# Attention beside an MLP on one core: where the transposed scores stand behind a value product

## The chip, the core and the metric

The kernel runs on one core of a Trainium2 chip. The metric is the device time of one execution in microseconds (us). Differences under about 0.2% (1.6 us) cannot be told from no change.

## What is computed

Inputs are float32: a sequence `x` of 2048 rows by 512 columns, attention weights for 32 heads of 16, and an MLP with 1792 hidden columns. The two branches are mixed by a gate computed for each row:

```
qkv = x @ wqkv                         # 32 heads, Dh = 16
scores = q k^T * Dh**-0.5              # row i sees columns i-255 .. i
a = (softmax(scores) @ v) @ wo
b = (silu(x @ w_gate) * (x @ w_up)) @ w_down
out = g * a + (1 - g) * b              # g = sigmoid(sum(x * gate_w)) per row
```

## The kernel before

Every float32 factor of the projections is split into a high and a low half, and three products of the halves are summed. The program has three stages: projections of q, k, v and a part of the MLP (0 to about 168 us); the attention stage, in which the rest of the MLP's gate and up products fill TensorE between the attention's own (about 168 to 633 us); and the output stage. The change lies in the second.

The 32 heads make 8 groups of four (`G`), the sequence 16 blocks of 128 rows (`NB`). The main loop runs over 128 slots `t`, one for each head group and key block, and each slot has four **places** `hd`. What stands in a place is written out by hand, and every engine executes its queue in that order:

- one **score** (`run(scores, 1)`, function `stage1`, L603): a matmul with 63 rows of weights into a PSUM bank of `pc` (three banks in turn, `pb1` among them), read by VectorE, which takes the row maximum for the next head group (L605).
- one **transposed score** (function `stage2`, L642) into a bank of `pd` (two banks in turn), read by ScalarE, which exponentiates it into `pt` (L644). GpSimd then masks pairs of them (L646, L649).
- some **steps** of the MLP products (`run(steps, n)`, function `lanes`, L564). A step is two matmuls with 64 rows of weights each, one on the upper and one on the lower half of TensorE's rows. Twelve steps complete a sum; ScalarE then copies it to `ev` (L511, function `copy_out`), in its own queue behind what the same place issued before.

A score and a transposed score use one half of the rows each: `r = slice(64 * j, ...)`, with `j` alternating from one to the next. `stage2` takes its heads in the order 1, 0, 3, 2 and the scores run one ahead, so that in a place of the kernel before both stand on the same half.

Every fourth slot has, after the steps of its second place, a **value product** (`av`, L664): 32 or 48 calls that multiply the exponentials of the last four to six key blocks by the values, into one bank of `pc` and one of `pd` (in the last head group two of `pc`). ScalarE copies the `pd` bank out (`ob`, L675) and VectorE the `pc` bank (`oe`, L681); after that the two banks go back into their turns. The table `DEAL` gives the steps of each place in the four slots from one value product's slot to the next.

Below, the 16 places of four slots are numbered 0 to 15, and such four slots are called a round. The value product stands at the end of place 1, and place 2 is the first behind it. T2 is the transposed score that the kernel before issues in place 2, T3 the next, and so on; the names stay with the scores in both kernels.

Of the kernel before, what the change touches and what calls it, by code (L numbers as in the profile page):

```python
# [19 lines left out]
NB = S // P  # L20
CH = 512
NCH = S // CH
G = H // 4
NF = F // P
VW = 4 * (DH + 1) + DH
NSLOT = 4
# [7 lines left out]
def gated_mix(ctx, tc, xT, xn, wqk, wv, wo, wgu, wd, gw, out):  # L34
# [52 lines left out]
    def run(gen, n=None):  # L87

        while n is None or n > 0:
            if next(gen, run) is run:  # L90
                break
            n = n and n - 1
# [19 lines left out]
    def bank(n):  # L112
        names = BANKS[n if isinstance(n, str) else ("pa", "pb", "pc", "pd")[n]]
        names.append(names.pop(0))
        return psum.tile([P, CH], F32, name=names[-1])
# [353 lines left out]
    with ExitStack() as A:  # L469
# [30 lines left out]
        def tick_end():  # L500
            for f in AT.pop(NOW[0], ()):
                f()
# [88 lines left out]
        def stage1(g, qb):  # L591

            hf, b = divmod(qb, NB // 2)
            if b == 0:
                MX[g, hf] = sm.tile([P, 4, NB // 2], F32, name="mx")
            q0, k0 = qb * P, max(0, qb - 2) * P
            n = q0 + P - k0
            for hd in range(4):
                pr, j = divmod(hd, 2)
                r = slice(64 * j, 64 * j + 63)  # L600

                ps = bank("pd") if g == 0 and pr else bank("pc")
                nc.tensor.matmul(ps[:, :n], QT[g % 2][pr][r, q0:q0 + P], KT[g % 2][pr][r, k0:k0 + n],  # L603
                                 start=True, stop=True)
                mx = nc.vector.tensor_tensor_reduce(out=ps[:, :n], in0=ps[:, :n], in1=mask[:, 3 * P - n:],  # L605
                                                    scale=1.0, scalar=NEG, op0=ALU.add, op1=ALU.max,
                                                    accum_out=MX[g, hf][:, hd, b:b + 1])
                if g == 0:
                    BEHIND.append(mx)
                yield  # L610

        def put_max(g, hf):

            mt = sm.tile([P, 32], F32R, name="mt", bufs=1)
            mtt = sm.tile([P, 32], F32, name="mtt", bufs=1)
            nc.vector.tensor_scalar(mt, MX[g, hf].rearrange("p h b -> p (h b)"), -1.0, None, op0=ALU.mult)
            nc.vector.transpose(mtt, mt.bitcast(F32))
            md = dram.tile([4, NB // 2, 4, 32], F32, name=f"md{g}{hf}")
            nc.sync.dma_start(md.rearrange("h b p q -> p (h b) q"), mtt)
            for pr in range(2):  # L620
                nc.sync.dma_start(halves_of(QT[g % 2][pr])[hf][63::64].bitcast(F32),
                                  md[2 * pr:2 * pr + 2].rearrange("h b p q -> h (b p q)"))
# [3 lines left out]
        def load_v(n):  # L626

            VG[n] = sm.tile([P, 4, VW], F32, name="vg", bufs=4)
            nc.sync.dma_start(VG[n], vd[n // 4, :, n % 4 * 4:n % 4 * 4 + 4])

        def stage2(g, kb):


            n = min(3, NB - kb) * P
            k0 = kb * P
            for hd in (1, 0, 3, 2):
                pr, j = divmod(hd, 2)
                r = slice(64 * j, 64 * j + 64)
                if j:
                    pt = PT[g, kb, pr] = ptp.tile([P, 2, 3 * P], F32, name="pt")  # L640
                ps = bank("pd")
                nc.tensor.matmul(ps[:, :n], KT[g % 2][pr][r, k0:k0 + P], QT[g % 2][pr][r, k0:k0 + n],  # L642
                                 start=True, stop=True)
                BEHIND.append(nc.scalar.activation(pt[:, j, :n], ps[:, :n], AF.Exp, scale=SCALE))  # L644
                if not j:
                    nc.gpsimd.affine_select(out=pt[:, :, :P], in_=pt[:, :, :P], pattern=[[0, 2], [1, P]],  # L646
                                            compare_op=ALU.is_ge, fill=0.0, base=0, channel_multiplier=-1)
                    if n == 3 * P:
                        nc.gpsimd.affine_select(out=pt[:, :, 2 * P:], in_=pt[:, :, 2 * P:],  # L649
                                                pattern=[[0, 2], [-1, P]], compare_op=ALU.is_ge, fill=0.0,  # L650
                                                base=-1, channel_multiplier=1)
                yield

        def av(g, c):

            AV[g, c] = bank("pc"), bank("pc" if g == G - 1 or g == G - 2 and c == NCH - 1 else "pd")

            orders = [[4 * c + m for m in ms if 4 * c + m >= 0] for ms in ((0, 1, 2, -1, -2, 3), (0, 1, -1, 2, 3, -2))]
            for n, kbs in enumerate(zip(*orders)):
                for j in range(4):  # L660
                    for h, (o, kb) in enumerate(zip(HALVES, kbs)):
                        k0 = kb * P + 64 * h
                        q0, q1 = max(k0, c * CH), min(k0 + W + 64, c * CH + CH)
                        nc.tensor.matmul(AV[g, c][h][32 * j:32 * j + 32, q0 - c * CH:q1 - c * CH],  # L664
                                         VG[4 * g + kb // 4][o, kb % 4, 17 * j:17 * j + 32],
                                         PT[g, kb, j // 2][o, j % 2, q0 - kb * P:q1 - kb * P],
                                         start=n == 0, stop=n == len(orders[0]) - 1, skip_group_check=True)

        def evacuate(g, c):

            first, second = AV[g, c]
            lo = 0 if c else 64
            e = osb.tile([P, CH], F32, name="oe", bufs=2)
            o = osb.tile([P, CH], F32, name="ob")
            nc.scalar.copy(o[:, lo:], second[:, lo:])  # L675
            if g == G - 1:
                nc.vector.tensor_tensor(out=e[:, lo:], in0=first[:, lo:], in1=o[:, lo:], op=ALU.add)
                if lo:
                    nc.vector.tensor_copy(e[:, :lo], first[:, :lo])
            else:  # L680
                nc.vector.tensor_copy(e, first)  # L681
                nc.gpsimd.tensor_tensor(out=e[:, lo:], in0=e[:, lo:], in1=o[:, lo:], op=ALU.add)  # L682
            later(4 if g == G - 1 else 0, lambda: nc.gpsimd.dma_start(od[g, :, c * CH:(c + 1) * CH], e))
# [73 lines left out]
        def tile_silu(n):  # L757
            (gt, up), sg = GOT[n], kept()
            TILE[n] = halves_of(pieces[TILE_AT[n]])
            nc.scalar.activation(sg, gt, AF.Silu)  # L760
            nc.vector.tensor_tensor(out=sg, in0=up, in1=sg, op=ALU.mult)
            yield
            split(*TILE[n], sg, nc.scalar, nc.vector)
# [38 lines left out]
            spread(4 * (16 * g + 9) + 3, 1, stack(g + 2, 0))  # L802
            spread(4 * (16 * g + 17) + 1, 1, stack(g + 2, 1))

        DEAL = [[[(hd + 1) * n // 4 - hd * n // 4 for hd in range(4)] for n in deal] for deal in ((5, 9, 8, 8), (8, 8, 8, 8))]
        DEAL[0][0] = 1, 2, 2, 0
        scores = chain(*(stage1(*divmod(b, NB)) for b in range(NB, G * NB)))
        run(scores, 1)
        for t in range(G * NB + 1):
            g, i = divmod(t, NB)  # L810
            d, part = divmod(t, NSLOT)
            s2 = stage2(g, i) if t < G * NB else iter(())
            values = part == 0 and t > 0
            if t == g7:
                BANKS["pc"].remove("pb1")
                BANKS["pd"].append("pb1")
            for hd in range(4):
                k = NOW[0] = NSLOT * t + hd
                run(scores, 1)
                if t < g7:  # L820
                    run(s2, 1)
                elif hd % 2 == 0:
                    run(s2, 2)
                if t == G * NB and hd == 0:
                    last_tile = tile_silu(2)
                    run(last_tile, 1)
                if t < G * NB:
                    run(steps, DEAL[t >= g7][part][hd])
                if hd == 1 and values:
                    av(*divmod(d - 1, NCH))  # L830
                    for f in LULL.pop(k, []) + UNDER:
                        f()
                    UNDER.clear()
                    evacuate(*divmod(d - 1, NCH))
                tick_end()
            if i in (7, 15) and g + 1 < G:
                UNDER.append(lambda g=g, i=i: put_max(g + 1, i // 8))
            if t >= 10 and t % 4 == 2 and t + 6 < G * NB:
                load_v((t + 6) // 4)
# [195 lines left out]
```

## Time and profile before

| what | value |
|---|---|
| median of 3 runs | 822.5 us (822.34 to 822.65) |
| the profiled execution's own time | 822.11 us |
| its span, first to last instruction | 820.4 us |
| busy: TensorE matmuls, weight loads | 812.0 us, 681.0 us |
| busy: VectorE, ScalarE, GpSimd | 550.4 us, 470.0 us, 402.1 us |
| granted TensorE clock | 1.00 |
| from the value product at 392.14 us to the next, at 405.09 us | 12.95 us |

PE is TensorE's matmul row and PEld its weight loads, DVE is VectorE, ACT ScalarE, POOL GpSimd. L603 is line 603 of the kernel. A tile's name in the profile is without its number. In a timeline a row gives the start, the duration, the engine, the line, and the tile written and read; in brackets stands how long the engine's queue was empty or held before it and what released it. Matmul durations run from the start to a modelled end and overlap with the next matmul's.

### The profile page before, as it was taken

Reading aid. Unit: us, or ns where it says so; the run is one execution under the profiler, and the core shown is the slowest. Engines: PE = TensorE matmul, PEld = TensorE weight load, DVE = VectorE, ACT = ScalarE, POOL = GpSimd, SP = SyncE. Lnnn points to the kernel's source line nnn. Section 1 sums busy time; section 2 is a strip of 40 time slices with the busy share of each in tenths; the row PEclk is TensorE's granted clock in tenths of the full one; section 3 lists DMA queues with packets and bytes.
Section 4 is the critical chain, followed back from the end, with each engine's and each line's share of the span. In section 5 each row is a group of like instructions: output and inputs, shape, how many; then the busy total and the mean of one; then the engine's idle time right before and its main releaser. Section 6 shows DMA issues by size and latency. Waiting matters only on the chain.

```text
span 820.4 us, 20498 instructions
## 1 busy us (share of the span) xinstructions
PE 812.0 (99%) x7681; PEld 681.0 (83%) x7681; DVE 550.4 (67%) x1425; ACT 470.0 (57%) x956; POOL 402.1 (49%) x715
## 2 busy tenths in 40 slices
PE   9999999999999999999999999999999999999997
PEld 7888888878888888888888888888887888888886
DVE  5675554248877888878888887786576666554652
ACT  7455553312576767767677676776776563435340
POOL 5124442260366666767667576665873205442320
PEclk9999999999999999999999999999999999999999
DMA  8446666385625654566555655352659997878611
GB/s 302 148 156 254 231 231 235 137 268 178 218 85 194 189 179 157 182 213 202 171 167 168 207 188 159 132 170 89 212 191 349 271 287 229 273 226 221 213 52 52
DMA packets 80211, 159.70 MB, mean 195 GB/s; under 512 B 14960, under 2 KB 19440, under 8 KB 80112
## 3 DMA queue, kind: packets, MB, share of 16 engines
q1 hardware_dynamic: 68544, 127.44, 47.5%
q0 software_dynamic: 10992, 29.91, 11.3%
q8 instruction: 60, 0.98, 0.5%
q10 hardware_dynamic: 576, 1.05, 0.4%
q14 instruction: 39, 0.32, 0.1%
HBM read 93.32 MB, written 65.01 MB: 193 GB/s over the span
## 4 chain that ended last, share of the span: by engine, by line
PE 95%; DMA 2%; DVE 1%; ACT 1%; POOL 0%; SPq 0%; issue 0%; DVEq 0%; ACTq 0%
PE pa L564 22%; PE pb L564 10%; PE pd L642 6%; PE pc L664 5%; PE pd L381 4%; PE pb L381 4%; PE pa L381 4%; PE pd L81 3%; PE pc L81 3%; PE pc L83 3%; PE pd L83 3%; PE pc L82 3%; PE pd L82 3%; PE pb L664 2%; PE pc L381 2%; PE pb L83 2%
## 5 line engine op out<-in xcount | busy, mean ns | idle before, releaser
L644 ACT ACTIVATE pt<-pd 128x384 f32<-128x384 f32 (+2 forms) x491 | 223.0, 474 | 43.9 <-PE pd L642 25.6
L605 DVE CUSTOM_DVE_ANT_0 pc<-pc,mask 128x384 f32<-128x384 f32 (+2 forms) x322 | 173.2, 548 | 23.5 <-PE pc L603 9.6
L642 PE MATMUL pd<-q,k 64*128 64x384 f32 (+2 forms) x491 | 167.2, 348 | 1.8 <-ACT pt L644 1.8
L564 PE MATMUL pa<-xhi,wh 64*128 64x512 f32 x492 | 168.5, 395 | 0.0
L564 PE MATMUL pa<-xlo,wh 64*128 64x512 f32 x492 | 167.6, 394 | 0.0
L564 PE MATMUL pa<-xhi,wl 64*128 64x512 f32 x492 | 165.9, 395 | 0.0
L646 POOL TENSOR_SCALAR_AFFINE_SELECT pt<-pt 128x256 f32<-128x256 f32 x256 | 110.9, 434 | 67.9 <-ACT pt L644 62.7
L642 PEld LDWEIGHTS pd<-q,k 64*128 64x128 f32 x491 | 90.8, 185 | 26.1 <-ACT pt L644 9.8
L603 PE MATMUL pc<-k,q 63*128 63x384 f32 (+2 forms) x322 | 106.9, 337 | 0.0
L564 PE MATMUL pb<-xhi,wl 64*128 64x512 f32 x244 | 96.2, 394 | 0.0
L564 PE MATMUL pb<-xhi,wh 64*128 64x512 f32 x244 | 96.2, 394 | 0.0
L564 PE MATMUL pb<-xlo,wh 64*128 64x512 f32 x244 | 96.2, 394 | 0.0
L649 POOL TENSOR_SCALAR_AFFINE_SELECT pt<-pt 128x256 f32<-128x256 f32 x224 | 94.3, 421 | 0.0
L605 DVE CUSTOM_DVE_ANT_0 pb<-pb,mask 128x384 f32<-128x384 f32 (+2 forms) x158 | 86.9, 550 | 6.9 <-PE pb L603 3.0
L564 PEld LDWEIGHTS pa<-xhi,wh 64*128 64x128 f32 x492 | 88.2, 185 | 1.9 <-DVE mx L605 0.5
L564 PEld LDWEIGHTS pa<-xhi,wl 64*128 64x128 f32 x492 | 87.0, 185 | 1.1
L564 PEld LDWEIGHTS pa<-xlo,wh 64*128 64x128 f32 x492 | 86.9, 185 | 0.6
L605 DVE DVE_READ_ACCUMULATOR2_ANT mx<- 128x1 f32 x512 | 72.8, 142 | 0.0
L921 DVE TENSOR_TENSOR sg<-got,sg 128x512 f32<-128x512 f32 x52 | 41.1, 790 | 45.2 <-ACT sg L920 39.4
L664 PE MATMUL pd<-pt,vg 64*32 64x320 f32 (+4 forms) x1184 | 63.1, 346 | 0.0
L603 PEld LDWEIGHTS pc<-k,q 63*128 63x128 f32 x322 | 58.6, 184 | 4.8 <-issue 4.3
L682 POOL TENSOR_TENSOR oe<-oe,ob 128x512 f32<-128x512 f32 (+1 forms) x28 | 35.2, 1256 | 54.5 <-ACT ob L675 51.5
(307 smaller groups left out, 2050.8 us busy)
## 6 DMA issues: line engine op xcount, KB each, us to landing
got<-raws SPq DMA_DIRECT2D x104, 256.0 KB
raws<-ev SPq DMA_DIRECT2D x91, 256.0 KB
q<-xd SPq DMA_DIRECT2D x96, 128.0 KB
k<-xd SPq DMA_DIRECT2D x96, 128.0 KB
xd<-cx SPq DMA_DIRECT2D x16, 512.0 KB
xd<-cy SPq DMA_DIRECT2D x16, 512.0 KB
od<-oe POOLq DMA_DIRECT2D x32, 256.0 KB, 3.4
raw<-wgu SPq DMA_DIRECT2D x25, 256.0 KB
```

The source lines that it names most:

```text
L81: nc.tensor.matmul(ps, lh, rh, start=start and i == 0, stop=False, skip_group_check=skip)
L82: nc.tensor.matmul(ps, lh, rl, start=False, stop=False, skip_group_check=skip)
L83: nc.tensor.matmul(ps, ll, rh, start=False, stop=stop and i == n - 1, skip_group_check=skip)
L381: nc.tensor.matmul(ps, l[:, w], r[:, k], start=n in (1, 2, 5) and k == m == 0, stop=k == 1 and m == 2, skip_group_check=True)
L564: mm = nc.tensor.matmul(ps[o], w[r], x[r], start=first and i == 0, stop=(o is odd or bool(lane)) and i == turn - 1)
L603: nc.tensor.matmul(ps[:, :n], QT[g % 2][pr][r, q0:q0 + P], KT[g % 2][pr][r, k0:k0 + n], start=True, stop=True)
L605: mx = nc.vector.tensor_tensor_reduce(out=ps[:, :n], in0=ps[:, :n], in1=mask[:, 3 * P - n:], scale=1.0, scalar=NEG, op0=ALU.add, op1=ALU.m ...
L642: nc.tensor.matmul(ps[:, :n], KT[g % 2][pr][r, k0:k0 + P], QT[g % 2][pr][r, k0:k0 + n], start=True, stop=True)
L644: BEHIND.append(nc.scalar.activation(pt[:, j, :n], ps[:, :n], AF.Exp, scale=SCALE))
L646: nc.gpsimd.affine_select(out=pt[:, :, :P], in_=pt[:, :, :P], pattern=[[0, 2], [1, P]], compare_op=ALU.is_ge, fill=0.0, base=0, channel_mu ...
L649: nc.gpsimd.affine_select(out=pt[:, :, 2 * P:], in_=pt[:, :, 2 * P:], pattern=[[0, 2], [-1, P]], compare_op=ALU.is_ge, fill=0.0, base=-1, ...
L664: nc.tensor.matmul(AV[g, c][h][32 * j:32 * j + 32, q0 - c * CH:q1 - c * CH], VG[4 * g + kb // 4][o, kb % 4, 17 * j:17 * j + 32], PT[g, kb, ...
```

## The change

```
-        DEAL = [[[(hd + 1) * n // 4 - hd * n // 4 for hd in range(4)] for n in deal] for deal in ((5, 9, 8, 8), (8, 8, 8, 8))]
-        DEAL[0][0] = 1, 2, 2, 0
+        DEAL = [[[(hd + 1) * n // 4 - hd * n // 4 for hd in range(4)] for n in deal] for deal in ((6, 8, 8, 8), (8, 8, 8, 8))]
+        DEAL[0][0] = 1, 2, 2, 1
         scores = chain(*(stage1(*divmod(b, NB)) for b in range(NB, G * NB)))
+        transposed = chain(*(stage2(*divmod(b, NB)) for b in range(G * NB)))
         run(scores, 1)
         for t in range(G * NB + 1):
...
-            s2 = stage2(g, i) if t < G * NB else iter(())
...
             for hd in range(4):
                 k = NOW[0] = NSLOT * t + hd
                 run(scores, 1)
                 if t < g7:
-                    run(s2, 1)
-                elif hd % 2 == 0:
-                    run(s2, 2)
+                    run(transposed, 0 if t and (part, hd) == (0, 2) else 2 if t > NSLOT and (part, hd) == (2, 1) else 1)
+                elif t < G * NB and hd % 2 == 0:
+                    run(transposed, 2)
```

The transposed scores become one stream over all slots. In place 2 none is issued, in place 9 two are, and between these each stands one place later than before. That holds in 27 rounds, those whose value product stands in slots 4 to 108; the last head group (from `g7`, slot 112) is dealt as before. The 30 steps of a round stay 30: place 3 gets one step where it had none, and place 7 two where it had three, so that places 3 to 6 have issued one step more than before when they end.

**TensorE behind a value product.** The rows begin with the first score behind the value product of slot 56. `pb1`, `pc0`, `pc1` are the score banks, `pd0` and `pd1` those of the transposed scores, `pa` and `pb0` those of the steps; the value product holds `pd1` here. Before:

```order
L603 MATMUL pb1_5776<-k01_1414,q01_1388 128x384
L642 MATMUL pd0_5780<-q11_1514,k11_1516 128x384
L564 MATMUL pa1_5696<-xhi0_91,wh_5522 128x512
L564 MATMUL pa0_5545<-xhi2_95,wh_5109 128x512
L564 MATMUL pa1_5696<-xlo0_92,wh_5522 128x512
L564 MATMUL pa0_5545<-xlo2_96,wh_5109 128x512
L603 MATMUL pc0_5787<-k00_1366,q00_1346 128x384
L642 MATMUL pd1_5790<-q11_1514,k11_1516 128x384
L603 MATMUL pc1_5795<-k00_1366,q00_1346 128x384
L642 MATMUL pd0_5799<-q10_1502,k10_1504 128x384
L564 MATMUL pa1_5696<-xhi0_91,wl_5523 128x512
L564 MATMUL pa0_5545<-xhi2_95,wl_5110 128x512
```

After:

```order
L603 MATMUL pb1_5776<-k01_1414,q01_1388 128x384
L564 MATMUL pa1_5696<-xhi0_91,wh_5518 128x512
L564 MATMUL pa0_5541<-xhi2_95,wh_5097 128x512
L564 MATMUL pa1_5696<-xlo0_92,wh_5518 128x512
L564 MATMUL pa0_5541<-xlo2_96,wh_5097 128x512
L603 MATMUL pc0_5783<-k00_1366,q00_1346 128x384
L642 MATMUL pd0_5787<-q11_1514,k11_1516 128x384
L564 MATMUL pa1_5696<-xhi0_91,wl_5519 128x512
L564 MATMUL pa0_5541<-xhi2_95,wl_5098 128x512
L603 MATMUL pc1_5794<-k00_1366,q00_1346 128x384
L642 MATMUL pd1_5797<-q11_1514,k11_1516 128x384
L564 MATMUL pa1_5696<-xhi0_91,wh_5518 128x512
```

T2 (`pd0_5780` before, `pd0_5787` after) moves from place 2 to place 3, and one step moves ahead of place 4; T3 goes into the bank of the value product in both. From here to place 8 a place's score and transposed score stand on different halves.

**TensorE at place 9.** The rows begin with the score of place 8 in the same round. Before, one transposed score in each place:

```order
L603 MATMUL pb1_5850<-k00_1366,q00_1346 128x384
L642 MATMUL pd0_5854<-q10_1502,k10_1504 128x384
L564 MATMUL pa0_5843<-xhi1_93,wl_5523 128x512
L564 MATMUL pb0_5619<-xhi3_97,wl_5110 128x512
L564 MATMUL pa0_5843<-xhi1_93,wh_5522 128x512
L564 MATMUL pb0_5619<-xhi3_97,wh_5109 128x512
L603 MATMUL pc0_5862<-k01_1414,q01_1388 128x384
L642 MATMUL pd1_5865<-q10_1502,k10_1504 128x384
L564 MATMUL pa0_5843<-xlo1_94,wh_5522 128x512
```

After:

```order
L603 MATMUL pb1_5845<-k00_1366,q00_1346 128x384
L642 MATMUL pd1_5848<-q11_1514,k11_1516 128x384
L564 MATMUL pa0_5839<-xhi1_93,wl_5519 128x512
L564 MATMUL pb0_5620<-xhi3_97,wl_5098 128x512
L564 MATMUL pa0_5839<-xhi1_93,wh_5518 128x512
L564 MATMUL pb0_5620<-xhi3_97,wh_5097 128x512
L603 MATMUL pc0_5858<-k01_1414,q01_1388 128x384
L642 MATMUL pd0_5862<-q10_1502,k10_1504 128x384
L642 MATMUL pd1_5865<-q10_1502,k10_1504 128x384
```

Place 8 now issues T7, and place 9 both T8 (`pd0_5862`) and T9 (`pd1_5865`), before its steps; from place 10 on the order is the old one.

**ScalarE in the same round.** The rows begin with the copy of the value product (`ob`); `pt<-pd` are the exponentials of T2, T3, ..., `ev` the copies of finished sums. Before:

```order
L675 COPY ob_5771<-pd1_5712 128x512
L644 ACTIVATE pt_5779<-pd0_5780 128x384
L644 ACTIVATE pt_5779<-pd1_5790 128x384
L644 ACTIVATE pt_5798<-pd0_5799 128x384
L511 COPY ev_5804<-pa0_5545 128x512
L644 ACTIVATE pt_5798<-pd1_5811 128x384
L644 ACTIVATE pt_5823<-pd0_5824 128x384
L644 ACTIVATE pt_5823<-pd1_5836 128x384
L644 ACTIVATE pt_5853<-pd0_5854 128x384
L644 ACTIVATE pt_5853<-pd1_5865 128x384
L511 COPY ev_5874<-pb0_5619 128x512
```

After:

```order
L675 COPY ob_5771<-pd1_5712 128x512
L644 ACTIVATE pt_5786<-pd0_5787 128x384
L511 COPY ev_5792<-pa0_5541 128x512
L644 ACTIVATE pt_5786<-pd1_5797 128x384
L644 ACTIVATE pt_5809<-pd0_5810 128x384
L644 ACTIVATE pt_5809<-pd1_5820 128x384
L644 ACTIVATE pt_5835<-pd0_5836 128x384
L644 ACTIVATE pt_5835<-pd1_5848 128x384
L644 ACTIVATE pt_5861<-pd0_5862 128x384
L644 ACTIVATE pt_5861<-pd1_5865 128x384
L511 COPY ev_5874<-pb0_5620 128x512
```

The first `ev` copy stood between T4 and T5 and now stands between T2 and T3, as its sum now ends in place 3 instead of 4. The other kind of round, which alternates with this one, has its first copy between T7 and T8 before and between T5 and T6 after (it ends in place 6 instead of 7). The second copies, in place 9 here and in place 12 there, follow the same exponential as before.

## The prediction

> **What bounds the kernel now.** I read the page first, then the attention stage by rounds, then who holds TensorE's queue there, and last the timeline behind one value product and in an undisturbed place.
>
> ```profile
> PE 812.0 (99%) x7681; PEld 681.0 (83%) x7681; DVE 550.4 (67%) x1425; ACT 470.0 (57%) x956; POOL 402.1 (49%) x715
> ```
> ```profile
> 392.14:405.09 12.95, 12.95 (x189) 10.86 (x188) 11.15 (x38) 9.22 (x21) 9.00 (x18) 1.00 0.47 149
> ```
> ```profile
> PEld pd L642 <- ACT pt L644: 5.6, 28, 0.4
> PEld pd L642 <- ACT ob L675: 5.2, 26, 0.2
> ```
>
> TensorE's row is full. The second row is one round (length; then busy time of PE, PEld, DVE, ACT and POOL, clock, DMA): VectorE is idle 1.8 us of 12.95, ScalarE 3.7 us, and the clock is 1.00. So matmul time sets the round, plus what TensorE's queue is held. The last two rows are of the waits in the attention stage (228 to 567 us; total, times, longest) and say by what: transposed scores wait for a `pd` bank, 26 times until the value product's copy `ob` is done, 28 times for an exponential. Here is TensorE behind one value product, then ScalarE and the weight loads at the same time:
>
> ```profile
> 407.57 0.44 PE L603 MATMUL pc<-k,q 63*128 63x384 f32 x1
> 407.58 0.50 PE L564 MATMUL pb<-xhi,wh 64*128 64x512 f32 x1
> 407.86 0.34 PE L642 MATMUL pd<-q,k 64*128 64x384 f32 x1
> 407.92 0.39 PE L564 MATMUL pb<-xlo,wh 64*128 64x512 f32 x1
> 408.03 0.39 PE L564 MATMUL pa<-xhi,wh 64*128 64x512 f32 x1
> 408.15 0.34 PE L603 MATMUL pb<-k,q 63*128 63x384 f32 x1
> 408.26 0.39 PE L564 MATMUL pa<-xlo,wh 64*128 64x512 f32 x1
> 408.40 0.44 PE L642 MATMUL pd<-q,k 64*128 64x384 f32 x1
> 408.50 0.40 PE L603 MATMUL pc<-k,q 63*128 63x384 f32 x1
> 408.80 0.44 PE L642 MATMUL pd<-q,k 64*128 64x384 f32 x1
> 408.80 0.50 PE L564 MATMUL pb<-xhi,wl 64*128 64x512 f32 x1
> ...
> 409.37 0.34 PE L603 MATMUL pc<-k,q 63*128 63x384 f32 x1
> ```
> ```profile
> 407.76 0.59 ACT L675 COPY ob<-pd 128x512 f32<-128x512 f32 x1 [2.06 <-PE pd L664]
> 408.25 0.50 ACT L644 ACTIVATE pt<-pd 128x384 f32<-128x384 f32 x1
> ```
> ```profile
> 408.40 0.18 PEld L642 LDWEIGHTS pd<-q,k 64*128 64x128 f32 x1 [0.18 <-ACT ob L675]
> 408.47 0.18 PEld L603 LDWEIGHTS pc<-k,q 63*128 63x128 f32 x1
> 408.80 0.18 PEld L642 LDWEIGHTS pd<-q,k 64*128 64x128 f32 x1
> 408.80 0.18 PEld L564 LDWEIGHTS pb<-xhi,wl 64*128 64x128 f32 x1
> ```
>
> And the spacings elsewhere, on TensorE, on ScalarE before and behind an `ev` copy, and in the weight loads behind that copy:
>
> ```profile
> 399.41 0.34 PE L642 MATMUL pd<-q,k 64*128 64x384 f32 x1
> ...
> 410.02 0.34 PE L603 MATMUL pb<-k,q 63*128 63x384 f32 x1
> 410.19 0.39 PE L564 MATMUL pa<-xhi,wh 64*128 64x512 f32 x1
> 410.19 0.34 PE L642 MATMUL pd<-q,k 64*128 64x384 f32 x1
> ...
> 410.65 0.33 PE L603 MATMUL pc<-k,q 63*128 63x384 f32 x1
> ```
> ```profile
> 399.78 0.49 ACT L644 ACTIVATE pt<-pd 128x384 f32<-128x384 f32 x1
> 400.26 0.59 ACT L511 COPY ev<-pb 128x512 f32<-128x512 f32 x1
> 400.74 0.50 ACT L644 ACTIVATE pt<-pd 128x384 f32<-128x384 f32 x1
> 401.12 0.49 ACT L644 ACTIVATE pt<-pd 128x384 f32<-128x384 f32 x1
> ...
> 410.63 0.49 ACT L644 ACTIVATE pt<-pd 128x384 f32<-128x384 f32 x1 [0.21 <-PE pd L642]
> ```
> ```profile
> 401.29 0.18 PEld L642 LDWEIGHTS pd<-q,k 64*128 64x128 f32 x1 [0.18 <-ACT pt L644]
> 401.29 0.29 PEld L564 LDWEIGHTS pa<-xlo,wh 64*128 64x128 f32 x2
> ```
>
> From these rows come all sizes below. On one half of TensorE's rows, what follows a 384-column matmul starts 0.17 to 0.18 us later (410.02 to 410.19) and what follows a 512-column one 0.23 later (408.03 to 408.26); a place with two steps takes 0.63 (410.02 to 410.65), and each half has six matmuls of 0.18, 0.18 and 4 x 0.23 in two places. An exponential starts 0.37 after its score (399.41 to 399.78; 0.44 from 410.19 to 410.63) and takes 0.49; queued behind another it starts 0.38 later (400.74 to 401.12), behind an `ev` copy 0.48 later (400.26 to 400.74). A held transposed score loads weights 0.05 after its bank is free (400.74 + 0.50 to 401.29), and a matmul that had nothing loaded ahead takes 0.10 to 0.11 more (0.44 against 0.34, 0.50 against 0.39). So a bank must be free about 0.16 before the score's turn. The two 401.29 rows, and the 408.80 ones, matter most: the steps' weights behind a held score wait with it, and on both halves (two loads at 401.29).
>
> **The change part by part.** Count from the first score behind the value product (407.57 = 0) and put matmuls loaded late at their effective start, 0.1 later.
>
> *The stall behind the value product goes.* Before, the half of place 3 does: step 0.12, step 0.35 (407.92), score 0.58 (408.15). T3 could follow at 0.76, but its bank was the value product's: `ob` ends at 408.35, T3 loads at 408.40 and counts from 0.94, 0.18 late. The next step could start at 1.12; it loads only with T4, which waits for T2's exponential (408.25 + 0.50), and counts from 1.34, 0.22 late. Together 0.40, and the score of place 5 comes at 1.80. After, that half does step 0.12, step 0.35, score 0.58, step 0.76, T3 0.99, two steps, score of place 5 at 1.62, with one step more (0.23) done: 0.41 gained. What is late next: T3 needs the same bank loadable by 0.88 and has it at 0.83. The other half does score, two steps, T2 at 0.75, step 0.92, score 1.15, two steps, T4 at 1.79. T2's exponential starts at 1.12 and ends at 1.61, so T4 can load at 1.66 to 1.73 (by the lag of 0.37 or 0.44) where 1.68 is wanted: 0.00 to 0.05, I take 0.03. No score takes a bank earlier than before by more than 0.18, and VectorE, idle 1.8 us in a round, covers that.
>
> *An `ev` copy comes between T2 and T3*, in every second round (13 of 27). Its sum ends with the step at 0.92 and its copy would start at about 1.35 (0.39 for the matmul, 0.05 for the signal); behind T2's exponential it starts at 1.50. T3's exponential, else at 1.50, starts at 1.98 and ends at 2.48. T5 needs that bank: its turn is 2.26 (score 1.62, steps 1.80 and 2.03), and it counts from 2.48 + 0.16 = 2.64, so 0.38 late. In the kernel before the same copy held T7 by a few hundredths; I take 0.03 back.
>
> *Place 9 issues T8 and T9.* T9 takes the bank of T7. Between their turns lie two steps, place 9's score and nothing more: 0.18 + 0.23 + 0.23 + 0.18 = 0.81 (T8 is on the other half). T7's exponential needs 0.37 + 0.49 + 0.16 = 1.02 even with ScalarE idle: T9 is 0.21 late (0.28 by the lag of 0.44). Behind T9 in TensorE's queue stand all steps of place 9, and by the 401.29 rows both halves wait. In the other 14 rounds an `ev` copy stands behind T5: the last step of its sum stands 0.57 behind T5's turn, so it starts at 0.57 + 0.39 + 0.05 = 1.0. With T6's turn at 0.80 and T7's at 1.27, it puts T6's exponential at 1.48 and T7's at 1.87 to 2.36; T9's turn is 2.08 and it counts from 2.52: 0.44 late. T10's wait behind that is under 0.05, and the second copies stand where they stood.
>
> *At nothing:* the step moved from place 7 to place 3 (its 0.23 is counted above on both sides), the different halves in places 3 to 8 (each half has the same matmuls in two places), GpSimd's masks and VectorE's row maxima, whose queues are idle 3.9 and 1.8 us of 12.95; the `raws` and weight DMAs that follow a copy start one place earlier. If GpSimd's cover were gone, the next value product would wait for a mask, which would show as a held L664.
>
> Sum by round: rounds with copies behind T2 and T9: -0.41 + 0.03 + 0.38 - 0.03 + 0.21 = +0.18. The others: -0.41 + 0.03 + 0.44 - 0.03 = +0.03. In all 13 x 0.18 + 14 x 0.03 = 2.8 us. The profiled execution took 822.1 us itself (span 820.4), 0.4 under the median of 822.5; 822.1 + 2.8 = 824.9, and I say **825.0**.
>
> By the Trainium skill (TensorE: Matmul & The Clock Gate, Part 3, The mechanism) TensorE's queue is a reorder window that pulls a weight load for other rows ahead of matmuls in flight. With it the steps of the free half would pass a held T9; the 401.29 rows speak against that for a score that waits for a semaphore, and the sum by the rule would be the second rival's.
>
> **The rivals.**
> - *The new waits are larger and meet the old ones.* If the bank of the value product comes 0.2 late for T3, because `ob` queues behind an `ev` copy, or the late exponentials of T8 and T9 hold T10 and T11 too, 0.2 of the gain is lost in each round: 824.9 + 27 x 0.2 = 830.3. For it: 28 waits for exponentials already; against it: ScalarE has 3.7 us in a round to recover.
> - *The double place is hidden: faster.* If the steps behind T9 run while it waits, its 0.21 and 0.44 vanish: 824.9 - 13 x 0.21 - 14 x 0.44 = 816.0. It decides from the point where weights of steps of place 9 are loaded ahead of T9's. For it: with nothing held the halves run beside each other (407.57 and 407.58); against it: 401.29.
> - *The two cancel.* With T9's waits smaller by 0.1, from a lag and a load that overlap more, 822.2: no change.
>
> **How the numbers follow.** A measurement of this kernel can tell about 0.2% (1.6 us) from no change, so faster is below 820.9 and slower above 824.1. The forecast (between 824.1 and 829.5) gets 0.50, the first rival 0.10, the hidden double place or a part of it that goes below 820.9 gets 0.18, and no change 0.22. The kernel not doing what it says has no share of its own: the order of instructions shows the moves, and a bank still late for T3 is in the first rival. The range leaves out 0.1 at either end: 819.0, some way into the hidden case, to 829.5.
>
> **What would show it.** Right: no wait of L642 for `ob`, and from the first score behind a value product to the fourth about 1.6 us instead of 1.80; in place 9 a load of `pd` held for an exponential, 27 times, with loads of steps at the same instant; in every second round another at T5, and the page's waits of L642 for L644 over 28. Wrong: rounds of 12.95 that fall to 12.6, steps that start in place 9 while T9 is held, or waits for `ob` still there.

## The result, and the profile after

The changed kernel takes 825.26 us (median of 6 runs, 824.90 to 828.47) against 822.42 us (822.07 to 822.75) for the kernel before beside it: a ratio of 1.0037, 95% interval 1.0020 to 1.0055. It is slower, by 2.8 us. The profiled execution took 825.3 us. Two executions among the experiments below, one of deal_copies (1128 us) and one of step_ahead (1604 us), stand far outside the others of their kernels and are left out of medians and ratios. First the page: span, and the busy time of each engine.

```profile
span 823.6 us, 20498 instructions
PE 815.4 (99%) x7681; PEld 683.6 (83%) x7681; DVE 547.6 (66%) x1425; ACT 468.6 (57%) x956; POOL 403.2 (49%) x715
```

The instructions are the same and TensorE's row is still full; its 3.4 us more are no work, since the row stays full while matmuls are held. Then the 27 rounds that the change touches, from the start of the first value product to the start of the twenty-eighth, as one stretch (length; busy time of PE, PEld, DVE, ACT, POOL; clock; DMA), before:

```profile
227.68:569.78 342.10, 342.10 (x4852) 290.53 (x4851) 276.68 (x947) 244.83 (x545) 227.83 (x476) 1.00 0.53 169
```

and after, followed by the round of the prediction's first row (12.95 us before) and the round behind it:

```profile
228.28:573.14 344.86, 344.85 (x4852) 292.95 (x4852) 272.15 (x947) 243.23 (x545) 229.27 (x476) 1.00 0.53 168
393.87:407.02 13.15, 13.15 (x189) 10.94 (x189) 10.97 (x38) 9.20 (x21) 9.07 (x18) 1.00 0.50 147
407.02:419.54 12.52, 12.52 (x189) 10.93 (x189) 10.12 (x38) 8.08 (x21) 7.40 (x16) 1.00 0.67 214
```

The stretch grew by 2.76 us at the same clock, where the whole span grew by 3.2 us (820.4 to 823.6): nearly all of the difference lies in it. Who is held there, from the waits between 228 and 567 us (total, times, longest):

```profile
PEld pd L642 <- ACT pt L644: 12.5, 60, 0.3
...
ACT pt L644 <- PE pc L603: 4.8, 20, 0.4
...
ACT pt L644 <- PE pb L603: 2.9, 11, 0.4
```

The row for `ob` (26 waits, 5.2 us) is gone, and that for exponentials has gone from 28 waits to 60. The two other rows are new: exponentials that are released by the end of a *score*, with which they have nothing to do. More on them below.

The starts of the scores on TensorE's row cut a round into places. Means of the lengths over 26 of these rounds (13 of either kind), in us, where "with one step more" marks the place of the moved step:

| scores of places | rounds with first copy in place 3: before, after | the other rounds: before, after |
|---|---|---|
| 2 to 5 (after: with one step more) | 1.79, 1.64 | 1.80, 1.68 |
| 5 to 7 | 1.26, 1.61 | 1.33, 1.28 |
| 7 to 9 (before: with one step more) | 1.55, 1.29 | 1.49, 1.28 |
| 9 to 11 | 1.26, 1.60 | 1.24, 1.65 |
| 11 to 16 | 3.25, 3.17 | 3.13, 3.17 |
| whole round | 12.92, 13.11 | 12.42, 12.44 |

**Behind the value product.** TensorE in the round that begins at 393.87, scores (L603) and transposed scores (L642) only:

```profile
396.36 0.44 PE L603 MATMUL pb<-k,q 63*128 63x384 f32 x1
...
396.92 0.34 PE L603 MATMUL pc<-k,q 63*128 63x384 f32 x1
...
397.11 0.33 PE L642 MATMUL pd<-q,k 64*128 64x384 f32 x1
...
397.33 0.36 PE L642 MATMUL pd<-q,k 64*128 64x384 f32 x1
397.51 0.34 PE L603 MATMUL pc<-k,q 63*128 63x384 f32 x1
...
398.00 0.34 PE L603 MATMUL pb<-k,q 63*128 63x384 f32 x1
398.17 0.34 PE L642 MATMUL pd<-q,k 64*128 64x384 f32 x1
...
398.89 0.44 PE L642 MATMUL pd<-q,k 64*128 64x384 f32 x1
```

ScalarE in the same round, from the copy `ob` to the copy in place 9 (x3 and x2: exponentials back to back):

```profile
396.55 0.59 ACT L675 COPY ob<-pd 128x512 f32<-128x512 f32 x1 [2.50 <-PE pd L664]
397.48 0.49 ACT L644 ACTIVATE pt<-pd 128x384 f32<-128x384 f32 x1 [0.35 <-PE pd L642]
397.87 0.58 ACT L511 COPY ev<-pa 128x512 f32<-128x512 f32 x1
398.33 1.53 ACT L644 ACTIVATE pt<-pd 128x384 f32<-128x384 f32 x3
400.10 1.04 ACT L644 ACTIVATE pt<-pd 128x384 f32<-128x384 f32 x2 [0.24 <-PE pc L603]
401.39 0.87 ACT L644 ACTIVATE pt<-pd 128x384 f32<-128x384 f32 x2 [0.25 <-PE pc L603]
```

And the loads of weights of T3, of T5 and of the step behind T5:

```profile
397.25 0.18 PEld L642 LDWEIGHTS pd<-q,k 64*128 64x128 f32 x1
...
398.89 0.18 PEld L642 LDWEIGHTS pd<-q,k 64*128 64x128 f32 x1
398.90 0.18 PEld L564 LDWEIGHTS pb<-xlo,wh 64*128 64x128 f32 x1
```

`ob` ends at 397.14, and T3 loads at 397.25 without waiting. From the first score to the fourth it is 398.00 - 396.36 = 1.64. T3's exponential stands behind the copy `ev` (398.33) and ends near 398.84, and T5 loads at 398.89, late (0.44 on TensorE's row instead of 0.34), with a step's load beside it.

**Place 9.** T6 to T9 and the scores of places 7 and 9 on TensorE's row, with the step behind T9, and T10:

```profile
399.47 0.33 PE L642 MATMUL pd<-q,k 64*128 64x384 f32 x1
399.63 0.34 PE L603 MATMUL pc<-k,q 63*128 63x384 f32 x1
...
400.28 0.33 PE L642 MATMUL pd<-q,k 64*128 64x384 f32 x1
...
400.74 0.34 PE L642 MATMUL pd<-q,k 64*128 64x384 f32 x1
400.92 0.34 PE L603 MATMUL pc<-k,q 63*128 63x384 f32 x1
401.19 0.44 PE L642 MATMUL pd<-q,k 64*128 64x384 f32 x1
401.19 0.50 PE L564 MATMUL pb<-xlo,wh 64*128 64x512 f32 x1
...
401.95 0.42 PE L642 MATMUL pd<-q,k 64*128 64x384 f32 x1
```

The loads of T9 and that step, and of T10:

```profile
401.19 0.18 PEld L642 LDWEIGHTS pd<-q,k 64*128 64x128 f32 x1 [0.32 <-ACT pt L644]
401.19 0.18 PEld L564 LDWEIGHTS pb<-xlo,wh 64*128 64x128 f32 x1
...
401.93 0.18 PEld L642 LDWEIGHTS pd<-q,k 64*128 64x128 f32 x1 [0.21 <-ACT pt L644]
```

T7 (400.28) has its exponential done at 401.14, where the pair that began at 400.10 ends; T9 loads 0.05 later, and the step of the other half with it. T10 is held as well (401.93), by T8's exponential: T8 started at 400.74, its exponential only at 401.39. On TensorE's row T10 then takes 0.42 instead of about 0.33, so it counts 0.10 late. Counted over the stretch (waits over 0.15 us), T9's load is held in all 27 rounds and T10's in the 13 with the first copy in place 3.

In the other kind of round the copy stands ahead of the exponentials of T6 to T9. ScalarE there, then the loads of T8, T9 and a step:

```profile
412.79 0.59 ACT L511 COPY ev<-pa 128x512 f32<-128x512 f32 x1
413.27 1.74 ACT L644 ACTIVATE pt<-pd 128x384 f32<-128x384 f32 x4
```
```profile
413.82 0.18 PEld L642 LDWEIGHTS pd<-q,k 64*128 64x128 f32 x1 [0.17 <-ACT pt L644]
414.20 0.18 PEld L642 LDWEIGHTS pd<-q,k 64*128 64x128 f32 x1 [0.20 <-ACT pt L644]
414.21 0.18 PEld L564 LDWEIGHTS pb<-xlo,wh 64*128 64x128 f32 x1
```

Four exponentials run without a gap behind the copy, and T8 and T9 are released one after the other, 0.38 apart.

### The profile page after: what moved, and what is told of

Same layout as the page of the kernel before. It is cut to its first block, busy times and chain, and to the rows that moved or that the text cites. A ratio compares the mean times of both kernels' runs of the same rounds, so it can differ in the third digit from the quotient of the medians.

```text
span 823.6 us, 20498 instructions
## 1 busy us (share of the span) xinstructions
PE 815.4 (99%) x7681; PEld 683.6 (83%) x7681; DVE 547.6 (66%) x1425; ACT 468.6 (57%) x956; POOL 403.2 (49%) x715
## 4 chain that ended last, share of the span: by engine, by line
PE 95%; DMA 2%; DVE 1%; ACT 1%; SPq 1%; issue 0%; DVEq 0%; ACTq 0%
PE pa L564 22%; PE pb L564 11%; PE pd L642 6%; PE pc L664 5%; PE pd L381 4%; PE pa L381 4%; PE pb L381 4%; PE pd L83 3%; PE pc L83 3%; PE pc L81 3%; PE pc L82 3%; PE pd L81 3%; PE pd L82 3%; PE pc L603 2%; PE pb L664 2%; PE pc L381 2%
## 5 line engine op out<-in xcount | busy, mean ns | idle before, releaser
L644 ACT ACTIVATE pt<-pd 128x384 f32<-128x384 f32 (+2 forms) x491 | 219.2, 475 | 48.5 <-PE pd L642 24.7
L642 PE MATMUL pd<-q,k 64*128 64x384 f32 (+2 forms) x491 | 164.2, 348 | 1.3 <-ACT pt L644 1.2
L564 PE MATMUL pa<-xhi,wl 64*128 64x512 f32 x492 | 163.3, 391 | 0.0
L646 POOL TENSOR_SCALAR_AFFINE_SELECT pt<-pt 128x256 f32<-128x256 f32 x256 | 111.6, 436 | 71.8 <-ACT pt L644 66.5
L642 PEld LDWEIGHTS pd<-q,k 64*128 64x128 f32 x491 | 90.2, 185 | 25.1 <-ACT pt L644 16.5
L603 PE MATMUL pc<-k,q 63*128 63x384 f32 (+2 forms) x322 | 105.6, 333 | 0.0
L649 POOL TENSOR_SCALAR_AFFINE_SELECT pt<-pt 128x256 f32<-128x256 f32 x224 | 94.4, 421 | 0.0
L564 PEld LDWEIGHTS pa<-xhi,wh 64*128 64x128 f32 x492 | 86.3, 185 | 1.7 <-DVE mx L605 0.5
L921 DVE TENSOR_TENSOR sg<-got,sg 128x512 f32<-128x512 f32 x52 | 44.5, 855 | 44.4 <-ACT sg L920 38.4
L603 PEld LDWEIGHTS pc<-k,q 63*128 63x128 f32 x322 | 58.6, 184 | 5.8 <-issue 4.3
```

What stands on the lines that cost most here:

```text
L564: mm = nc.tensor.matmul(ps[o], w[r], x[r], start=first and i == 0, stop=(o is odd or bool(lane)) and i == turn - 1)
```

## The experiments

The stages outside the 27 rounds took 478.3 to 482.3 us in the profiled executions, so beside the median time and its ratio the stretch of these rounds in the profiled execution is given (342.10 us before, 344.86 after). The one kernel that was profiled twice, deal_copies, gave 336.56 and 336.60 us. Times of the kernel before on the same chips: 823.2 (first four), 823.4 (second four) and 823.0 us (last three).

| experiment | us | ratio, 95% interval | stretch, us |
|---|---|---|---|
| deal_only | 821.7 | 0.9983 (0.9969 to 0.9997) | 340.17 |
| skip_only | 828.7 | 1.0070 (1.0052 to 1.0087) | 347.60 |
| copy_late | 824.0 | 1.0014 (1.0000 to 1.0029) | 342.14 |
| room | 825.7 | 1.0034 (1.0019 to 1.0049) | 344.13 |
| score_behind | 823.8 | 0.9999 (0.9985 to 1.0013) | 342.23 |
| room_copies | 826.3 | 1.0035 (1.0023 to 1.0047) | 344.14 |
| room_place1 | 830.9 | 1.0084 (1.0050 to 1.0117) | 348.57 |
| deal_copies | 817.9 | 0.9932 (0.9910 to 0.9955) | 336.56 |
| deal_copies_again | 818.5 | 0.9942 (0.9926 to 0.9957) | 336.60 |
| step_ahead | 820.3 | 0.9961 (0.9947 to 0.9975) | 338.80 |
| step_14 | 818.2 | 0.9944 (0.9929 to 0.9959) | 336.77 |

**The two parts alone.** The change deals a step to place 3, and it skips and doubles transposed scores. deal_only is the kernel before with the first part:

```diff
-        DEAL = [... for deal in ((5, 9, 8, 8), (8, 8, 8, 8))]
-        DEAL[0][0] = 1, 2, 2, 0
+        DEAL = [... for deal in ((6, 8, 8, 8), (8, 8, 8, 8))]
+        DEAL[0][0] = 1, 2, 2, 1
```

> The steps dealt 6, 8, 8, 8 and 1, 2, 2, 1 as in the change, the transposed scores one in each place as before. Theory of the prediction (waits for pd banks in ScalarE's queue): T3 still waits 0.18 us for the value product's bank, but the step that now stands in place 3 fills the time in which T4 waited for T2's exponential (0.22 us); in rounds whose first copy stands in place 3 it comes between T3 and T4 and holds T6 by about 0.2 us, so those gain 0.05 and the others 0.22 us: 822.4 - 14 x 0.22 - 13 x 0.05 = 818.7 us. Rival A (only the copy that comes a place earlier costs, the double place nothing): 13 x 0.2 us slower, 825 us. Rival B (the different halves of TensorE's rows in places 3 to 8 cost): nothing changes, 822.4 us.

skip_only is the changed kernel with the two old lines.

> The transposed scores skip place 2 and stand twice in place 9 as in the change, the steps dealt 5, 9, 8, 8 and 1, 2, 2, 0 as before. Theory: without the step in place 3, T3 comes earlier and still waits 0.18 us for the value product's bank, T4 0.2 us for T2's exponential, half of the old stall; T9 waits 0.21 us where its round has its first copy in place 4, and 0.37 us where the copy of place 7 stands between T6 and T7: +0.14 and -0.02 us in a round, 824.2 us. Rival A: the copies stand where they stood, so the gain of 0.2 us in 27 rounds stays, 817 us. Rival B: as slow as the whole change, 825.3 us.

The parts nearly add up: the deal moves the stretch by 340.17 - 342.10 = -1.9, the skip by 347.60 - 342.10 = +5.5, together +3.6 where the change has +2.8. So the skip, which was to help, is what costs. Scores of places 2 to 5 take 1.64 there in the rounds with the first copy in place 4, 0.15 less than before, and scores of places 9 to 11 take 1.67 in these and 1.62 in the others, about 0.4 more than before. Its waits, in which T9 is held in each round:

```profile
PEld pd L642 <- ACT pt L644: 12.6, 44, 0.4
```

The time expected (824.2) was too low by about 4 us: without the extra step the gain behind the value product is smaller, and the transposed scores of places 9 and 10 cost 0.4 in both kinds of round.

deal_only has its step for nothing behind the value product (scores of places 2 to 5: 1.80 with one step more, against 1.79). But most of it is given back, because the sums end one place earlier, and with them their copies: in the rounds with the copy in place 3 it stands ahead of T4's exponential now, and scores of places 5 to 7 take 1.50 instead of 1.26; in the others scores of places 9 to 11 take 1.34 instead of 1.24.

**The copy behind T2.** copy_late is the changed kernel, with the copy that ends in place 3 put one place later into ScalarE's queue:

```diff
-            soft(0, lambda: nc.scalar.copy(place, ps))
+            soft(1 if 16 < NOW[0] < 4 * (G - 1) * NB and NOW[0] % 16 == 3 else 0, lambda: nc.scalar.copy(place, ps))
```

> The whole change, and the copy of a sum that ends in place 3 is issued one place later, so that it stands behind T3's exponential and not between T2's and T3's. Theory: T5's wait of 0.38 us goes in 13 rounds, 825.3 - 4.9 = 820.4 us, and no load of place 6 is held there. Rival A: the same and a little more, under 820.4 us. Rival B: 825.3 us.

T5's wait is gone: scores of places 5 to 7 take 1.25 where they took 1.61. That is nearly the whole of the predicted +0.38, caused by the copy. But the stretch fell by 2.7 and not by 13 x 0.36 = 4.7 us: scores of places 9 to 11 take 1.68 instead of 1.60, and places 11 to 16 have lost most of their gain (3.22 instead of 3.17). With T5's wait gone, T7 starts ahead of the score of its place and not behind it, and its exponential comes 0.56 behind T7's start instead of 0.37 (medians of these rounds); the experiment on late signals takes this up.

**Steps ahead of T9.** room is the changed kernel with three steps instead of two in places 8 and 9, and one in places 10 and 13:

```diff
+        DEAL[0] = (1, 2, 2, 1), (2, 2, 2, 2), (3, 3, 1, 2), (2, 1, 2, 2)
```

> The whole change, with 3 steps in places 8 and 9 and 1 in places 10 and 13 (in place of 2 in each), so that T7 to T9 and T8 to T10 lie one step, 0.23 us, further apart. Theory: T9's wait of 0.21 us goes in 13 rounds and falls by 0.23 us in 14, 825.3 - 2.7 - 3.2 = 819.4 us. Rival A (the double place costs nothing): 825.3 us. Rival B: 825.3 us.

T9's load is held in 2 of the 27 rounds instead of all, and scores of places 9 to 11, with the steps they had before, take 1.36 and 1.42 instead of 1.60 and 1.65. So T9's wait was real and was decided by the steps between T7 and T9. T10's load is still held in 12 of the 13 rounds of the first kind. The time did not follow: the stretch fell by 0.7. In the round that begins at 392.9 the load of the transposed score of place 12 is held now:

```profile
402.47 0.18 PEld L642 LDWEIGHTS pd<-q,k 64*128 64x128 f32 x1 [0.31 <-ACT pt L644]
```

Places 12 and 15 take 0.83 and 0.87 there, against 0.66 and 0.63 after the change. Two places behind a place that gave a step up stands a wait: at place 12 in all rounds of the first kind (in none after the change), at place 15 in 10 of the 26. Places 11 to 16, with a step (0.23) less, take 3.24 and 3.07 against 3.17 and 3.17: 0.30 and 0.13 are lost there, against the 0.24 and 0.23 gained in places 9 to 11.

**The late signals.** score_behind is copy_late with the transposed score ahead of the score in places 3 to 8:

```diff
+                n2 = 0 if t and (part, hd) == (0, 2) else 2 if t > NSLOT and (part, hd) == (2, 1) else 1
+                ahead = NSLOT < t < g7 and 3 <= 4 * part + hd < 9 or t == NSLOT and hd == 3
+                if ahead:
+                    run(transposed, n2)
                 run(scores, 1)
                 if t < g7:
-                    run(transposed, 0 if t and (part, hd) == (0, 2) else 2 if t > NSLOT and (part, hd) == (2, 1) else 1)
+                    run(transposed, 0 if ahead else n2)
```

> copy_late, and in places 3 to 8 the transposed score stands ahead of the place's score in TensorE's queue. In copy_late T7 began before the score of place 8, which is ahead of it in the queue, and its exponential began 0.56 us after it and not 0.37, right after that score's end. Theory (a matmul's end is signalled in the order of the queue): with T7 ahead its exponential begins 0.37 to 0.43 us after it, and T9's load is held about 0.15 us less in the rounds whose copies stand in places 3 and 9; 2 us faster than copy_late if T9 sets those rounds, unchanged if T10's wait behind it does. Rival (ScalarE itself was late): 0.56 us and the hold stay.

T7 and the score of place 8 in copy_late, and T9's load there:

```profile
398.72 0.34 PE L642 MATMUL pd<-q,k 64*128 64x384 f32 x1
398.87 0.34 PE L603 MATMUL pb<-k,q 63*128 63x384 f32 x1
```
```profile
399.82 0.18 PEld L642 LDWEIGHTS pd<-q,k 64*128 64x128 f32 x1 [0.35 <-ACT pt L644]
```

The same in score_behind:

```profile
398.87 0.33 PE L642 MATMUL pd<-q,k 64*128 64x384 f32 x1
398.89 0.34 PE L603 MATMUL pb<-k,q 63*128 63x384 f32 x1
```
```profile
399.78 0.18 PEld L642 LDWEIGHTS pd<-q,k 64*128 64x128 f32 x1 [0.29 <-ACT pt L644]
```

From T7's start to T9's load it is 1.10 in copy_late and 0.91 in score_behind: 0.19 less. So the order of the queue, not T7's own start, decides when its exponential begins. Scores of places 9 to 11 take 1.60 in the first kind of round, as after the change, instead of 1.68. But the rounds are none the shorter (342.23 against 342.14): T8, in place 9, still stands behind its score, T10 is held, and scores of places 5 to 7 take 0.1 more.

**Room and late copies together.** room_copies takes the steps of places 8 and 9 from place 1, ahead of the value product, and puts four copies one place later; room_place1 has that deal and leaves the copies.

```diff
+        DEAL[0] = (1, 0, 2, 1), (2, 2, 2, 2), (3, 3, 2, 2), (2, 2, 2, 2)
...
-            soft(0, lambda: nc.scalar.copy(place, ps))
+            soft({4: 1, 7: 1, 9: 1, 12: 1}.get(NOW[0] % 16, 0) if 16 < NOW[0] < 4 * (G - 1) * NB else 0, lambda: nc.scalar.copy(place, ps))
```

> The whole change, with 3 steps in places 8 and 9, taken from place 1 (ahead of the value product, where no transposed score follows closely), and the copies of sums that end in places 4, 7, 9 and 12 issued one place later. Theory: T7 to T9 and T8 to T10 lie 1.04 us apart where 1.02 is needed, and no copy stands between two exponentials that a near score waits for, so the gain of 0.38 us behind the value product is kept in most of the 27 rounds: 0.25 to 0.30 us each, 814 to 816 us, with few loads of L642 held. Rival A' (room with 1 step in places 10 and 13 was slow because the double place costs by itself, not by the new short places): 824 us or more. Rival B (different halves): 825 us.

> room_copies with the copies where the sums end (places 4, 9 and 7, 12). Theory: the copy of place 7 stands between T6's and T7's exponentials and holds T9 by 0.3 to 0.4 us in 14 rounds, which room_copies does not have: 4 to 5 us over it, 820 to 821 us. If the room alone counts: as room_copies.

Both missed by far. room_copies' waits:

```profile
PEld pd L642 <- ACT pt L644: 3.2, 14, 0.4
PEld pd L664 <- ACT pt L644: 2.6, 13, 0.3
```

The waits of transposed scores have nearly gone in room_copies, but without steps in place 1 the value product itself waits for an exponential, in these two kernels alone, and in room_copies 2.60 us pass from its start to the first score behind it instead of 2.32. That is 0.28 more in each of 27 rounds, or 7.5 us, of which the waits for exponentials are 2.6; what makes the rest is not shown. The late copies are worth 348.57 - 344.14 = 4.4 us in this pair.

**The deal with late copies.** If the skip costs and the step gains, and copies that come too early take most of the gain, then the kernel before with the new deal and the copies of places 3 and 6 one place later should beat both:

```diff
+        DEAL[0] = (1, 2, 2, 1), (2, 2, 2, 2), (2, 2, 2, 2), (2, 2, 2, 2)
...
+            soft({3: 1, 6: 1}.get(NOW[0] % 16, 0) if 16 < NOW[0] < 4 * (G - 1) * NB else 0, lambda: nc.scalar.copy(place, ps))
```

> deal_only, and the copies of sums that end in places 3 and 6 issued one place later. Theory: T6's wait of about 0.2 us in the rounds with a copy in place 3 goes, and the one of T8 behind the copy in place 6, 0.1 us, in the others: 13 x 0.2 + 14 x 0.1 = 4 us less than deal_only, 817 us. If the copies are not what holds T6 and T8: as deal_only, 821 us.

> The new deal in the order of the transposed scores of before, with the copies of places 3 and 6 one place later, timed once more beside the two that build on it: 818.3, with 27 rounds in 336.6 us.

Its stretch and its waits:

```profile
227.60:564.16 336.56, 336.56 (x4853) 285.35 (x4852) 278.04 (x947) 243.54 (x545) 227.09 (x476) 1.00 0.55 172
```
```profile
PEld pd L642 <- ACT pt L644: 7.0, 37, 0.4
PEld pd L642 <- ACT ob L675: 5.2, 26, 0.2
```

It does, twice: 5.5 us less in 27 rounds, 0.20 in a round (12.72 and 12.21 against 12.92 and 12.42), nearly the 0.23 of the step that now fills T4's wait.

**What is left behind the value product.** T3 still waits for `ob`. step_ahead is deal_copies with the step of place 3 dealt to place 2, ahead of T3; step_14 has that step besides, and one less in place 14 (first and second line):

```diff
+        DEAL[0] = (1, 2, 3, 0), (2, 2, 2, 2), (2, 2, 2, 2), (2, 2, 2, 2)
+        DEAL[0] = (1, 2, 3, 1), (2, 2, 2, 2), (2, 2, 2, 2), (2, 2, 1, 2)
...
+            soft({2: 2, 6: 1}.get(NOW[0] % 16, 0) if 16 < NOW[0] < 4 * (G - 1) * NB else 0, lambda: nc.scalar.copy(place, ps))
```

> The same with the step of place 3 dealt to place 2 (1, 2, 3, 0), so that it stands ahead of the place's score and of T3; the copy of that sum keeps its place. My theory: what is left behind a value product is T3 waiting for the bank of the value product, 26 waits of 0.2 us, and one step's time (0.23) ahead of T3 covers it without a skipped score. 27 rounds lose 0.15 each, 332.5 us, time 814. If T4's wait for the exponential of T2 takes its place (T2 starts no earlier, so T4 cannot either), the waits for ob go and the rounds stay: 336.5 us, 818.

> As in step_ahead, but place 3 keeps its step and place 14 gives one up (1, 2, 3, 1 and 2, 2, 1, 2): places 2 to 13 have issued one step more. If T4 is what comes late next, this one is faster than step_ahead by up to 0.2 in a round, 331 to 333 us, since T4 then has a step more ahead of it, less what the place with one step costs (the transposed score of place 15 held by an exponential, 0.2 in some rounds). If T4 isn't late, it is no faster than step_ahead.

My theory fell, and so did its rival (T4): in step_ahead the waits for `ob` are gone, and those for exponentials have grown from 37 to 49, of which T5 has 24, where it had 3:

```profile
PEld pd L642 <- ACT pt L644: 10.9, 49, 0.4
```

Scores of places 2 to 5 take 1.79 as before, and places 5 to 7 take 1.35 and 1.40 instead of 1.27 and 1.33: it is 2.2 us slower than deal_copies. step_14 does its extra step behind the value product for 0.04 (1.83 and 1.86), gives 0.20 back at places 5 and 6 in the first kind of round (1.47 against 1.27), and in the others 0.19 at places 11 to 15 (3.12 with one step less, against 3.16): level with deal_copies.

## Why the prediction was right

The terms came out as follows, in us per round, from the table of places (rounds with the first copy in place 3, then the others):

| step of the prediction | predicted | measured |
|---|---|---|
| behind the value product, T4's wait with it | -0.38, -0.38 | 1.64 - 1.79 - 0.23 = -0.38; 1.68 - 1.80 - 0.23 = -0.35 |
| T5 behind the copy | +0.38, 0 | +0.35, -0.05 |
| places 7 and 8, without the moved step | -0.03, -0.03 | 1.29 - 1.55 + 0.23 = -0.03; 1.28 - 1.49 + 0.23 = +0.02 |
| place 9 | +0.21, +0.44 | +0.33, +0.41 |
| places 11 to 15 | 0 | -0.08, +0.04 |
| places 0 and 1 and the value product | 0 | +0.01, -0.05 |
| round | +0.18, +0.03 | +0.19, +0.02 |

- *The stall behind the value product* goes as worked out, to a hundredth: T2 0.75 behind the first score (397.11), its exponential at 1.12 (397.48), the copy at 1.51, T3's exponential at 1.97, T5 effective at 2.63 where 2.64 was said. But the skip was given credit that is the step's: skip_only has 0.15 of it alone, and deal_only fills T4's wait without any skip.
- *T5's wait*: +0.35 for +0.38, and copy_late shows that the copy is its cause. That each term could be taken back by itself was not said, but later expected of copy_late, and is wrong: of 4.7 us removed 2.7 were gained.
- *T9*: its turn would have been 400.28 + 0.81 = 401.09 and it counts from 401.29 (its load at 401.19 and 0.10): 0.20 late, 0.21 said. The step that failed is "T10's wait behind that is under 0.05". By the lag of 0.37, T8's exponential would have started at 401.11 and T10 could have loaded at 401.65; it started at 401.39, behind the end of the score, and T10 loaded at 401.93 and counts 0.10 late. T9's 0.20 and this 0.10 make nearly all of the +0.33, of which places 11 to 15 give back 0.08. In the other rounds T9's term was +0.41 for +0.44, and T8 was held too, which the sum did not have apart.
- *The rivals.* The new waits did not meet in the way that would cost 0.2 in each round. The double place was not hidden: the step's load at 401.19 starts with T9's and not ahead of it. The Trainium skill (TensorE: Matmul & The Clock Gate, Part 3, The mechanism) has weight loads for other rows pulled ahead of matmuls in flight; here, behind a load that waits for a semaphore, the trace shows none that is.
- The sum landed closer than its terms, and that is luck: in 13 rounds, 0.12 too little at place 9 was offset by the 0.08 given back and 0.03 too much at T5; in the others, the terms up to place 15 come to +0.07, and 0.05 less at places 0 and 1, which nothing here explains, brings them to +0.02.
- *At nothing*: the different halves, which T8 in place 9 has as well, were not nothing. A transposed score that starts ahead of its place's score can have its exponential late (31 are released by a score, none before), and by T8's this holds T10. As for GpSimd, by the waits, the value product's loads wait for GpSimd's masks (L646, L649) 9 times, 3.3 us in all, before and after alike.

Why does skip_only lose 0.41 at places 9 and 10 in the rounds in which the change loses 0.33, and copy_late 0.42? Neither has T5's wait, and in both T7 starts ahead of the score of place 8 and has its exponential 0.53 to 0.56 behind its start. After the change T7 starts behind that score (400.28 and 400.10), with 0.37. In score_behind, without T5's wait but with T7 ahead in the queue, it is 0.37 again and the loss is 0.33. So the difference goes with the late signal of T7. What stays open is why score_behind gains nothing in all, and why T10 is held there in 13 rounds and in copy_late in one.

## What to carry to other kernels

A wait on a ring of two banks is a property of the work between two uses of a bank: put matmul work that is ready anyway between them, as the step in place 3 does, rather than moving the producers, which must catch up somewhere and pay there. When work is moved between places, look at what its completion triggers on other queues: copies that came one place earlier took two thirds of the gain, and putting them back one place was worth 3.6 us. And when several waits follow each other on one such ring, don't add up their removals: copy_late, room and step_ahead each removed the wait they aimed at and got a part of it, or nothing, as other uses of the ring were late instead.

## What the runs showed of the hardware

A matmul that runs ahead on a free half of the rows is reported no sooner than the one issued ahead of it. T8 stands behind the score of place 9 in the queue, starts 0.18 before it (400.74 and 400.92), and its exponential starts at 401.39, 0.65 behind T8 and 0.47 behind the score, released by the score (`<-PE pc L603`); T6 and the score of place 7 do the same (399.47, 399.63, exponential at 400.10). Where the transposed score stood ahead of the score, in score_behind, T7's exponential came 0.19 sooner after T7's start. The kernel before, in which both stand on one half, has no exponential released by a score in the 27 rounds, the change 31 with 7.7 us; the experiments in the old order have 0 to 6, those with the skip 8 to 32. The Trainium skill (TensorE: Matmul & The Clock Gate, Part 3, The mechanism) says that matmuls start and end in the order of the program; the trace agrees for the ends as far as the exponentials show them, and for the starts, across the two halves, it shows the opposite, by 0.15 to 0.18 us.
